# Another order for the head, the first tile's groups and the float32 pairs of a two-stage feed-forward kernel with chunked attention

## The chip, the cores and the metric

The kernel runs on one core of one Trainium2 chip. The metric is the device time of one execution in microseconds; lower is better. The profile names the engines PE (TensorE), PEld (its weight loads), DVE (VectorE), ACT (ScalarE), POOL (GpSimd) and SP (SyncE, which issues all the DMAs here).

## What is computed

The reference computes attention within chunks of 64 positions, then two feed-forward blocks on the 4608 rows of 512 that it gives:

```
scores = scale * q_c @ k_c^T, per chunk of 64, head of 64
attn = exp(scores - max) / (sum + 1e-9);  x = attn @ v_c
h = x @ w_in;  x2 = (h * cos(h)) @ w_out            (512 -> 2048 -> 512)
out = (((x2 @ w1) * (x2 @ w2)) @ w3) @ w_out2       (512 -> 1024 -> 1024 -> 512)
```

Everything is float32. The kernel splits each float32 operand of a large matmul into a rounded high part and a low part, and forms a product by three matmuls (high by high, high by low, low by high: `mm3`, lines 102 to 104).

## The kernel before

**Tiles and groups.** The 4608 rows are nine tiles of 512 (`NTILE`), and a tile is four attention blocks of 128 rows (`j`, 36 in all). The 2048 columns of h are taken 256 at a time, eight groups (`G1`). Pass 0 does groups 0 to 4 (`GA`) of every tile in turn and pass 1 the rest. The loop runs over `groups`, with index i: i = 0 to 4 is the first tile, i = 5 to 9 the second, and so on.

**A group.** For a group the kernel computes h in two halves, d and e (`stepP` and `stepQ` for the first two tiles, a seven-product scheme `Seven` later). Each half goes through a chain: a rounded copy on ScalarE (`chain_t`, line 524), a remainder on VectorE (`chain_r`, 529), absolute value and sine on ScalarE (`chain_cos`, 534 and 535), and the product h * cos(h) on VectorE (`chain_g`, 539). The next group splits this product into high and low parts (`split_g`: ScalarE, then GpSimd, 547 and 548) and multiplies it by w_out into four accumulators (`x2_mm`, in two halves e = 0 and e = 1). So group i runs the second product of group i - 1.

**The order of a group** is written out by hand in a string. Each letter is one step and every engine gets its instructions in that order: P, Q (or 1, 2, 5, 3) are the halves of h, a and c the copies, A and C the remainders, b and d the sines, B and D the products, s the split, x and y the halves of the second product, v one conversion slot, q one attention step, L, M, H, R the steps of a float32 pair, o the split of an attention tile into an operand. `ORDER0` holds for i = 0 to 3, `ORDER0E` for i = 4, `ORDER1P` and `ORDER1PE` for i = 5 to 9, later strings after that. `START` orders the head the same way: A, B, E, C, D with a block's number are its attention steps, x is a conversion slot, o an operand's split.

**Attention.** A block has five steps: A, scores on TensorE and maximum and subtraction on VectorE (`att_scores`, 343 to 347); B, the exponential on ScalarE (353); E, sums and scaling (358 to 362; the scaling is on VectorE in the head, on GpSimd later); C, four transposes and their copy `pt` (369, 371); D, the values and their copy into `xf` (383, 387). The tile `qk` has two buffers and so has the tag `ex`, which the exponentials `ex` and the copies `pt` share; `vt` has one. Step A of block j first issues the loads of q and k of block j + 1, step D those of v. The head runs blocks 0 to 3, and groups 0 to 3 of a tile run one block each of the next tile.

**Weights.** The twenty weight blocks of groups 0 to 4 come as 64-bit numbers, 512 KB each. `conv_tick` moves a pipeline by one slot: it loads a raw block two slots ahead, prepares one (`conv_a`, 120 to 122), adds the parts of another (`conv_b`, 128) and rounds and splits a third (`conv_c`, 173, and the low part at 195). Three raw buffers are in turn. One slot is about four VectorE instructions. A block is usable three slots after its preparation began, and `need` in the loop before each group makes sure that the slots so far cover what the group reads: slot t gives block t - 4, and group i needs the blocks 4i and 4i + 1 of w_in, and 2 and 3 behind them one group later.

**Float32 pairs.** From the third tile on, h uses sums and differences of weight blocks. `conv_b` stores the float32 form of w_in to the array `wr`; `sum_load` reads a pair of blocks back (207), `sum_make` forms four sums on VectorE (216 to 219), `sum_hi` and `sum_lo` split them (224, 228). There are five pairs. Before, L issues a load only when no pair is under way, and the next group's M makes it, so that a load stands one group's end ahead of its use.

Of the kernel before, what the change touches and what calls it, by code (L numbers as in the profile page):

```python
# [21 lines left out]
NJ = NT // P  # L22
# [3 lines left out]
GA = 5  # L26
# [5 lines left out]
SCALE = 0.125  # L32


START = "A0 x x A1 B0 E0 x B1 C0 E1 D0 C1 A2 x D1 A3 B2 E2 o o C2 B3 E3 D2 C3 x D3 o o"

ORDER0 = "PsvqQqacvAqCxvqbBdyvDq"
ORDER0E = "PsvQacvACxobBodyDoo"
ORDER1P = "PsqMhQqqHaclAxqbCrRmBdyqDL"
ORDER1PE = "SPsQacATCoobBoxodoDyoo"  # L40
ORDER1 = "1s2qMh5qqHa3clAxqbCrRmBdyqDL"
# [11 lines left out]
def chunk_attention_two_ffn(  # L53
# [96 lines left out]
    def new_w(key):  # L150
        W[key] = t = wpool.tile([P, 2, TT], F32R, tag=f"w{take(slots, key)}", name="w")
        return t
# [46 lines left out]
        return True  # L199


    sp = {}

    def sum_load(g):
        pair = ("in", g)
        sp["at"] = pair, new_w((pair, 2))
        nc.sync.dma_start(out=f32(W[pair, 2]), in_=wr[g])

    def sum_make():
        assert not held[0] and not held[1]  # L210
        held[1] = True
        pair, w = sp["at"]
        a, m = f32(w[:, 0]), f32(w[:, 1])
        a11, a12, a21, a22 = a[:, 0:256], a[:, 256:512], m[:, 0:256], m[:, 256:512]
        s2, s3, s4, s1 = spare[:, 0, 0:256], spare[:, 0, 256:512], spare[:, 1, 0:256], spare[:, 1, 256:512]
        nc.vector.tensor_tensor(out=s3, in0=a11, in1=a21, op=ALU.subtract)
        nc.vector.tensor_tensor(out=s1, in0=a21, in1=a22, op=ALU.add)
        nc.vector.tensor_tensor(out=s2, in0=s1, in1=a11, op=ALU.subtract)
        nc.vector.tensor_tensor(out=s4, in0=a12, in1=s2, op=ALU.subtract)
        sp["parts"] = [(W[pair, 1][:, :, 0:256], s1), (w, spare[:, 0]), (new_s4((pair, 3)), s4)]  # L220
# [5 lines left out]
    def sum_lo():  # L226
        for d, x in sp.pop("parts"):
            nc.vector.tensor_tensor(out=d[:, 1], in0=x, in1=f32(d[:, 0]), op=ALU.subtract)
        sp.pop("at")
        held[1] = False  # L230

    def need(*keys):
# [88 lines left out]
    def bank(early):  # L321
        return (ps_h.tile([P, 512], F32, tag="h", name="ps_ah") if early
                else ps_at.tile([P, 512], F32, tag="at", name="ps_at"))

    def load_qk(j):
        qks[j] = t = wk.tile([P, 2, 2 * HP, 64], F32, tag="qk", name="qk")
        nc.sync.dma_start(out=t[:, 0], in_=q[j])
        nc.sync.dma_start(out=t[:, 1], in_=k[j])
# [3 lines left out]
        nc.sync.dma_start(out=vt, in_=v[j])  # L332

    def att_scores(j, early):
        if j + 1 < NJ:
            load_qk(j + 1)
        qk = qks.pop(j)
        ps = ps_at.tile([P, 512], F32, tag="at", name="ps_s")
        s3 = ps.rearrange("p (h k) -> p h k", k=64)
        for h in range(2 * HP):  # L340
            for c in range(2):
                r = slice(64 * c, 64 * c + 64)
                nc.tensor.matmul(s3[r, h], qk[r, 0, h], qk[r, 1, h], start=True, stop=True)  # L343
        mx = small.tile([P, 2 * HP], F32, tag="mx", name="mx")
        nc.vector.reduce_max(out=mx, in_=s3, axis=AX.X)
        ex = wk.tile([P, 2 * HP, 64], F32, tag="ex", name="ex")
        nc.vector.tensor_tensor(out=ex, in0=s3, in1=mx.unsqueeze(2).to_broadcast([P, 2 * HP, 64]),
                                op=ALU.subtract)
        att[j] = ex
# [324 lines left out]

    with tc.manual_schedule():
        load_qk(0)
        for g in range(GA):
            cq.extend((nm, 2 * g + e) for nm in ("in", "out") for e in range(2))
        conv_tick()
# [4 lines left out]
        plain = ["B11", "B21", "T1", "B22"]  # L684
        for tok in START.split():
            if tok == "x":
# [6 lines left out]
        def order_of(i, nth, end):  # L693
            if i < GA:
                return ORDER0E if end else ORDER0
            if i < 2 * GA:
# [10 lines left out]
        n_sums = 0  # L707
        fq = 0
        for i in range(NG):
            if i == GA:  # L710
                sq.extend(("wo2", j) for j in range(FB2))
                for g in range(GA, G1):
                    sq.extend((nm, 2 * g + e) for nm in ("in", "out") for e in range(2))
                    lq.extend((("in", g), p_) for p_ in range(4))
                    lq.extend(("out", 2 * g + e) for e in range(2))
                lq.extend(("wo2", j) for j in range(FB2))
                sq.extend(("w3", j) for j in range(N3))
                for f in range(FB2):
                    sq.extend((nm, f) for nm in ("w1", "w2"))
                    if N3 + f < 16:  # L720
                        sq.append(("w3", N3 + f))
                    lq.extend((("w12", f), p_) for p_ in range(4))
                st_load()
            if i == iB + FOLD - 1:
                load_w3()
                load_w3()
            ps, n, g = groups[i]
            k_tile = (i - iB) // (G1 - GA)
            nth = (g, g - GA)[ps]
            end = g == (GA, G1)[ps] - 1  # L730

            def load_x(op):
                nc.sync.dma_start(out=f32(X[op]), in_=xs[k_tile][op])

            need(*((("in", g), p_) for p_ in range(2 if i < 2 * GA else 4)))
            z = Plain(("in", g)) if i < 2 * GA else Seven(
                ("in", g), (bank_h,) * 4, False, load_x if ps and end and k_tile in xs else None)
            if i:
                need(*(("out", 2 * groups[i - 1][2] + e) for e in range(2)))
            n_q = n_o = n_l = 0  # L740
            for op in order_of(i, nth, end):
                if op == "s" and i:
                    split_g(i - 1)
                elif op == "x" and i:
                    x2_mm(i - 1, 0)
                elif op == "y" and i:
                    x2_mm(i - 1, 1)
                elif op == "v":
                    conv_tick()
                elif op == "L":  # L750
                    if n_sums < GA and not sp:
                        sum_load(n_sums)
                        n_sums += 1
                elif op in "MHR":
                    if sp:
                        {"M": sum_make, "H": sum_hi, "R": sum_lo}[op]()
                elif op == "l":
                    n_l += 1
                    nxt = sq[sat[1]][0] if sat[1] < len(sq) else None
                    if ps == 0 or nxt == ("w1" if nth else "w3" if n_l > 1 else "w2"):  # L760
                        st_low()
                elif op == "m":
                    st_bits()
                elif op == "h":
                    st_hi()
                elif op == "r":
                    st_lo()
                elif op in "1253PQ":
                    getattr(z, "step" + op)()
                elif op in "ac":  # L770
                    chain_t(i, z.d if op == "a" else z.e, "ac".index(op))
                elif op in "AC":
                    chain_r(i, z.d if op == "A" else z.e, "AC".index(op))
                elif op in "bd":
                    chain_cos(i, "bd".index(op))
                elif op in "BD":
                    chain_g(i, z.d if op == "B" else z.e, "BD".index(op))
                elif op == "q":
                    if i < iA and nth < 4:
                        att_tok(steps[20 * n + 5 * nth + n_q], False)  # L780
                    elif i >= iB + FOLD and fq < 4 * FB2:
                        need(("w3", fq // 2), *(("wo2", j) for j in range(FB2)))
                        fold(fq // 4, fq % 4)
                        fq += 1
                    n_q += 1
                elif op in "ST":
                    x_sums("ST".index(op))
                elif op == "o":
                    if i < GA and not n_o:
                        x_plain()  # L790
                    x_op((z.done if i < GA or i >= 2 * GA else OPS)[n_o], n + 1 if ps == 0 else None)
                    n_o += 1
            if i >= iA:
                pump()
            if n == (NTILE - 1, NTILE - 2)[ps]:
                done_with((("in", g), p_) for p_ in range(4))
            if ps == 1:
                if nth == 0 and k_tile not in xs:
                    nc.sync.dma_start(out=xf, in_=xd[k_tile] if k_tile + 1 < NTILE else x2d[order[0]])
                if nth == 1:  # L800
                    for c in range(CC):
                        load_x2a(n, c)
# [78 lines left out]
```

## Time and profile before

| | |
|---|---|
| median of 3 runs | 1572.31 us (1569.95 to 1574.7) |
| profiled execution, device time | 1572.75 us |
| its span | 1571.0 us |
| mean granted TensorE clock | 0.982 |
| busy: PE, DVE, ACT, POOL | 96%, 70%, 49%, 17% of the span |
| first P (h of group 0) starts | 37.91 us |
| P of group 4 starts | 115.50 us |

The profiled execution is one run of the program; its device time is 1.75 us more than its span, which runs from the first to the last instruction. Each engine works through its own instructions in order, and waits at an instruction until what it needs is there. The idle time in brackets at a row of a timeline is that wait, with what ended it. An engine's share of busy time is a mean over stages that have different limits; what a change of one stage is worth is read in that stage.

### The profile page before, as it was taken

What the parts mean: (1) busy time and instruction counts of PE and PEld (TensorE: products, weight loads), DVE (VectorE), ACT (ScalarE), POOL (GpSimd) and SP (SyncE); (2) the same over time, 40 slices, a digit from 0 to 9 for tenths busy, and PEclk for the clock granted to TensorE, in tenths of its full rate; (3) what the DMA queues carried; (4) which work ended last, traced back from release to release, by engine and by line L of the source; (5) the groups of instructions that cost most, each with busy time, mean ns of one, the idle gap of its engine ahead of it and who ended that gap; (6) DMA issues with size and microseconds to landing.
All of it is one profiled execution on the core that took longest, in us unless ns stands there. A gap on an engine that the chain in (4) does not pass through costs nothing.

```text
span 1571.0 us, 28515 instructions
## 1 busy us (share of the span) xinstructions
PE 1505.1 (96%) x11340; PEld 1360.7 (87%) x11340; DVE 1105.3 (70%) x1804; ACT 771.9 (49%) x1313; POOL 263.6 (17%) x206
## 2 busy tenths in 40 slices
PE   4789989999999999999999999899999999999998
PEld 4678878888888888978889888799999999999998
DVE  5875687888888877788777776556646656566464
ACT  3666777878878776555555554312212212212121
POOL 0122212222222222221222222110000000000000
PEclk8889999999999999999999999999999999999999
DMA  6644463665646544956887887931001011011000
GB/s 202 200 145 142 152 221 127 229 210 188 225 169 211 200 130 169 363 185 218 296 292 279 281 285 255 406 114 54 21 34 55 1 54 55 1 54 42 14 28 27
DMA packets 98629, 248.80 MB, mean 158 GB/s; under 512 B 10944, under 2 KB 13760, under 8 KB 96832
## 3 DMA queue, kind: packets, MB, share of 16 engines
q1 hardware_dynamic: 98496, 246.98, 44.8%
q8 instruction: 89, 1.46, 0.4%
q14 instruction: 44, 0.36, 0.1%
HBM read 151.78 MB, written 95.16 MB: 157 GB/s over the span
## 4 chain that ended last, share of the span: by engine, by line
PE 82%; DVE 7%; DMA 5%; ACT 3%; issue 1%; SPq 1%; POOL 0%; DVEq 0%; ACTq 0%; POOLq 0%
PE acc L102 11%; PE acc L103 11%; PE ps_hh L102 11%; PE acc L104 10%; PE ps_hh L104 10%; PE ps_hh L103 10%; PE ps_aa L103 5%; PE ps_aa L102 5%; PE ps_aa L104 5%; PE ps_s L343 2%; PE ps_at L383 2%; DMA w<-sd 1%; PE ps_at L369 1%; DMA xf<-xd 1%; DMA w<-wr 1%
## 5 line engine op out<-in xcount | busy, mean ns | idle before, releaser
L548 POOL TENSOR_TENSOR g<-t,g 128x512 fp32r<-128x512 f32 x144 | 198.4, 1399 | 610.8 <-ACT g L547 514.0
L102 PE MATMUL acc<-g,w 128*128 128x512 f32 x576 | 231.9, 403 | 0.0
L103 PE MATMUL acc<-g,w 128*128 128x512 f32 x576 | 229.1, 398 | 0.1
L104 PE MATMUL acc<-g,w 128*128 128x512 f32 x576 | 228.4, 396 | 0.0
L97 ACT ACTIVATE phl<-e 128x512 fp32r<-128x512 f32 x72 | 45.5, 632 | 364.8 <-DVE e L646 356.7
L466 DVE TENSOR_TENSOR d<-x,ps_hh 128x512 f32<-128x512 f32 x134 | 91.8, 685 | 159.1 <-PE ps_hh L104 107.5
L102 PE MATMUL ps_hh<-T,w 128*128 128x256 f32 x680 | 196.5, 289 | 0.3 <-ACT x L458 0.3
L103 PE MATMUL ps_hh<-T,w 128*128 128x256 f32 x680 | 193.2, 284 | 0.0
L104 PE MATMUL ps_hh<-T,w 128*128 128x256 f32 x680 | 193.1, 284 | 0.0
L102 PE MATMUL ps_hh<-B,w 128*128 128x256 f32 x656 | 189.4, 289 | 2.9 <-DVE t L539 1.8
L103 PE MATMUL ps_hh<-B,w 128*128 128x256 f32 x656 | 186.1, 284 | 0.0
L104 PE MATMUL ps_hh<-B,w 128*128 128x256 f32 x656 | 186.0, 284 | 0.0
L102 PEld LDWEIGHTS ps_hh<-B,w 128*128 128x128 f32 x656 | 125.9, 192 | 10.1 <-DVE t L539 2.5
L102 PEld LDWEIGHTS ps_hh<-T,w 128*128 128x128 f32 x680 | 131.1, 193 | 3.3 <-ACT x L458 0.6
L103 PEld LDWEIGHTS ps_hh<-T,w 128*128 128x128 f32 x680 | 131.2, 193 | 0.6
L104 PEld LDWEIGHTS acc<-g,w 128*128 128x128 f32 x576 | 110.4, 192 | 24.0
L104 PEld LDWEIGHTS ps_hh<-T,w 128*128 128x128 f32 x680 | 131.2, 193 | 0.0
L103 PEld LDWEIGHTS ps_hh<-B,w 128*128 128x128 f32 x656 | 126.0, 192 | 4.4
L102 PEld LDWEIGHTS acc<-g,w 128*128 128x128 f32 x576 | 111.1, 193 | 20.3
L103 PEld LDWEIGHTS acc<-g,w 128*128 128x128 f32 x576 | 110.8, 192 | 20.5 <-POOL g L548 0.6
L104 PEld LDWEIGHTS ps_hh<-B,w 128*128 128x128 f32 x656 | 125.9, 192 | 0.0
L103 PE MATMUL ps_aa<-T,w 128*128 128x256 f32 x432 | 122.4, 283 | 0.4 <-DVE T L98 0.4
(136 smaller groups left out, 3618.9 us busy)
## 6 DMA issues: line engine op xcount, KB each, us to landing
w<-sd SPq DMA_DIRECT2D x63, 512.0 KB, 7.7
sd<-raw SPq DMA_DIRECT2D x104, 256.0 KB, 2.4
qk<-in_q_dram SPq DMA_DIRECT2D x36, 256.0 KB, 4.8
qk<-in_k_dram SPq DMA_DIRECT2D x36, 256.0 KB, 4.7
vt<-in_v_dram SPq DMA_DIRECT2D x36, 256.0 KB, 2.9
x2a<-x2o SPq DMA_DIRECT2D x36, 256.0 KB, 2.5
x2a<-x2a SPq DMA_DIRECT2D x36, 256.0 KB, 6.3
x2d<-x2a SPq DMA_DIRECT2D x36, 256.0 KB, 4.7
```

Of the source, the lines that this page charges most:

```text
L97: nc.scalar.activation(dst[:, 0], src, AF.Copy)
L102: nc.tensor.matmul(ps, a[0], b[0], start=first, stop=False)
L103: nc.tensor.matmul(ps, a[0], b[1], start=False, stop=False)
L104: nc.tensor.matmul(ps, a[1], b[0], start=False, stop=last)
L343: nc.tensor.matmul(s3[r, h], qk[r, 0, h], qk[r, 1, h], start=True, stop=True)
L369: nc.tensor.transpose(ps[:, P * h:P * h + P], ex[:, 2 * h:2 * h + 2].rearrange("p e k -> p (e k)"), ident)
L383: nc.tensor.matmul(o[r, h, t], vt[r, c, h], pt[r, h, t], start=True, stop=True)
L466: nc.vector.tensor_tensor(out=two(self.d), in0=self.x1.unsqueeze(1).to_broadcast([P, 2, 256]), in1=two(p26), op=ALU.add)
L548: nc.gpsimd.tensor_tensor(out=lo, in0=r, in1=f32(hi), op=ALU.subtract)
```

## The change

1. **Head.** q and k of blocks 0 and 1 are both loaded before the first conversion slot. In the head, step A of block j loads up to block j + 2, and it issues that load after its matmuls. `START` puts A of block 1 right after A of block 0, and A of block j + 2 before D of block j; it has four conversion slots instead of five.
2. **First tile's groups.** In `ORDER0` the chain of d (a, A) stands before Q, the attention step A and the second conversion slot come after it, y follows x directly, one conversion slot stands between the two products and one at the group's end, and the attention steps C and D come after x and y. `ORDER0E` puts a and A before Q and y behind x likewise.
3. **Float32 pairs.** `ORDER0E` ends with L; loads no longer wait for the pair under way (`loaded` is a list), and M makes a pair when it is two groups past the one whose number it has. Every pair is made in the same group as before, and is loaded a group earlier.

```diff
-START = "A0 x x A1 B0 E0 x B1 C0 E1 D0 C1 A2 x D1 A3 B2 E2 o o C2 B3 E3 D2 C3 x D3 o o"
-ORDER0 = "PsvqQqacvAqCxvqbBdyvDq"
-ORDER0E = "PsvQacvACxobBodyDoo"
+START = "A0 A1 x B0 E0 B1 C0 x E1 A2 D0 C1 x B2 E2 A3 D1 C2 o o B3 E3 D2 C3 x D3 o o"
+ORDER0 = "PsvaAqQvqcCqxybBdvDqvq"
+ORDER0E = "PsvaAQvcCxybBodDoooL"
...
-    sp = {}
+    sp, loaded = {}, []
...
     def sum_load(g):
         pair = ("in", g)
-        sp["at"] = pair, new_w((pair, 2))
+        loaded.append((g, pair, new_w((pair, 2))))
         nc.sync.dma_start(out=f32(W[pair, 2]), in_=wr[g])
...
-        pair, w = sp["at"]
+        _, pair, w = loaded.pop(0)
...
     def att_scores(j, early):
-        if j + 1 < NJ:
-            load_qk(j + 1)
         qk = qks.pop(j)
...
                 nc.tensor.matmul(s3[r, h], qk[r, 0, h], qk[r, 1, h], start=True, stop=True)
+        while qk_at[0] < min(NJ, j + 2 + early):
+            load_qk(qk_at[0])
...
         load_qk(0)
+        load_qk(1)
...
                 elif op == "L":
-                    if n_sums < GA and not sp:
+                    if n_sums < GA:
                         sum_load(n_sums)
                         n_sums += 1
-                elif op in "MHR":
+                elif op == "M":
+                    if loaded and i > GA + loaded[0][0]:
+                        sum_make()
+                elif op in "HR":
                     if sp:
-                        {"M": sum_make, "H": sum_hi, "R": sum_lo}[op]()
+                        {"H": sum_hi, "R": sum_lo}[op]()
```

The strings move instructions in three places that matter below.

SyncE's queue at the very start, before (qk, raw and vt are the tiles of q and k, of a raw weight block and of v; the line numbers of the changed kernel are two or three higher):

```order
L327 DMA qk_175<-in_q_dram 128x512
L328 DMA qk_175<-in_k_dram 128x512
L112 DMA raw_178<-in_w_in_dram 128x1024
L112 DMA raw_180<-in_w_in_dram 128x1024
L332 DMA vt_187<-in_v_dram 128x512
L327 DMA qk_189<-in_q_dram 128x512
L328 DMA qk_189<-in_k_dram 128x512
L112 DMA raw_217<-in_w_out_dram 128x1024
L130 DMA wr0_149<-cw_213 128x512
L112 DMA raw_225<-in_w_out_dram 128x1024
```

and in the changed kernel:

```order
L329 DMA qk_175<-in_q_dram 128x512
L330 DMA qk_175<-in_k_dram 128x512
L329 DMA qk_178<-in_q_dram 128x512
L330 DMA qk_178<-in_k_dram 128x512
L112 DMA raw_181<-in_w_in_dram 128x1024
L112 DMA raw_183<-in_w_in_dram 128x1024
L334 DMA vt_190<-in_v_dram 128x512
L329 DMA qk_209<-in_q_dram 128x512
L330 DMA qk_209<-in_k_dram 128x512
L329 DMA qk_233<-in_q_dram 128x512
L330 DMA qk_233<-in_k_dram 128x512
L112 DMA raw_244<-in_w_out_dram 128x1024
```

q and k of the second block move ahead of the two raw blocks of w_in, and those of the third and fourth ahead of the first raw block of w_out.

VectorE in group 1, from the sums of its attention block on, before (t is the chain's tile, ps_hh a half of h, cw and w a weight block in conversion):

```order
L358 TENSOR_REDUCE sm_744<-ex_700 128x8
L359 TENSOR_SCALAR sm_744<-sm_744 128x8
L361 RECIPROCAL rc_747<-sm_744 128x8
L529 SCALAR_TENSOR_TENSOR t_730<-ps_hh_702,t_730 128x512
L128 ISA cw_736<-raw_614,cw_736 128x1024
L121 TENSOR_SCALAR cw_770<-raw_676 128x512
L122 SCALAR_TENSOR_TENSOR cw_770<-raw_676,cw_770 128x512
L195 TENSOR_TENSOR w_767<-cw_671,w_767 128x512
L539 TENSOR_TENSOR t_728<-t_728,ps_hh_637 128x512
L128 ISA cw_770<-raw_676,cw_770 128x1024
L121 TENSOR_SCALAR cw_804<-raw_741 128x512
L122 SCALAR_TENSOR_TENSOR cw_804<-raw_741,cw_804 128x512
```

and in the changed kernel, from the remainder of e on:

```order
L531 SCALAR_TENSOR_TENSOR t_731<-ps_hh_694,t_731 128x512
L360 TENSOR_REDUCE sm_734<-ex_692 128x8
L361 TENSOR_SCALAR sm_734<-sm_734 128x8
L363 RECIPROCAL rc_737<-sm_734 128x8
L541 TENSOR_TENSOR t_667<-t_667,ps_hh_627 128x512
L128 ISA cw_723<-raw_605,cw_723 128x1024
L121 TENSOR_SCALAR cw_777<-raw_665 128x512
L122 SCALAR_TENSOR_TENSOR cw_777<-raw_665,cw_777 128x512
L195 TENSOR_TENSOR w_773<-cw_660,w_773 128x512
L541 TENSOR_TENSOR t_731<-t_731,ps_hh_694 128x512
L128 ISA cw_777<-raw_665,cw_777 128x1024
L121 TENSOR_SCALAR cw_795<-raw_728 128x512
```

Before, a whole conversion (lines 128, 121, 122, 195) stands between the remainder of e and the product of d. Now that product follows the sums directly, one conversion stands between the two products, and another begins right behind the second.

SyncE's queue around the first float32 pair, from the end of group 4 on, before (wr_149 is the first pair's float32 form, wr_150 the second's):

```order
L332 DMA vt<-in_v_dram 128x512
L389 DMA xd_82<-xf 128x2048
L112 DMA raw<-in_wo_dram 128x1024 x2
L327 DMA qk<-in_q_dram 128x512
L328 DMA qk<-in_k_dram 128x512
L573 DMA x2a_131<-x2o 128x512 x4
L332 DMA vt<-in_v_dram 128x512
L207 DMA w<-wr_149 128x1024
L327 DMA qk<-in_q_dram 128x512
```

and in the changed kernel:

```order
L334 DMA vt<-in_v_dram 128x512
L391 DMA xd_82<-xf 128x2048
L207 DMA w<-wr_149 128x1024
L112 DMA raw<-in_wo_dram 128x1024 x2
L329 DMA qk<-in_q_dram 128x512
L330 DMA qk<-in_k_dram 128x512
L575 DMA x2a_131<-x2o 128x512 x4
L334 DMA vt<-in_v_dram 128x512
L207 DMA w<-wr_150 128x1024
```

The load of the first pair moves from behind the end of group 5 to the end of group 4.

## Rows read from the trace of the kernel before

**Rows 1.** The page, busy time of each engine with its share of the span.

```profile
PE 1505.1 (96%) x11340; PEld 1360.7 (87%) x11340; DVE 1105.3 (70%) x1804; ACT 771.9 (49%) x1313; POOL 263.6 (17%) x206
```

**Rows 2.** TensorE's timeline, head: start us, length us, engine, line, tiles, count, [idle before <-releaser].

```profile
4.19 1.97 PE L343 MATMUL ps_s<-qk 64*64 64x64 f32 x32 [4.19 <-DMA qk<-in_k_dram]
...
10.70 1.97 PE L343 MATMUL ps_s<-qk 64*64 64x64 f32 x32 [4.54 <-DMA qk<-in_k_dram]
...
16.03 1.09 PE L369 MATMUL ps_ah<-ident,ex 128*128 128x128 f32 x4 [3.36 <-DVE ex L362]
...
29.63 1.09 PE L369 MATMUL ps_ah<-ident,ex 128*128 128x128 f32 x4 [3.75 <-DVE ex L362]
...
36.00 1.97 PE L383 MATMUL ps_ah<-pt,vt 64*64 64x64 f32 x32 [1.01 <-DMA vt<-in_v_dram]
...
37.91 0.58 PE L102 MATMUL ps_hh<-B,w 128*128 128x256 f32 x1
```

**Rows 3.** The same timeline in groups 0 to 4.

```profile
50.56 1.12 PE L369 MATMUL ps_at<-ident,ex 128*128 128x128 f32 x4 [4.79 <-POOL ex L362]
...
55.63 0.58 PE L102 MATMUL ps_hh<-B,w 128*128 128x256 f32 x1 [1.30 <-DVE t L539]
...
89.44 0.66 PE L369 MATMUL ps_at<-ident,ex 128*128 128x128 f32 x4 [3.41 <-POOL ex L362]
...
115.50 0.38 PE L102 MATMUL ps_hh<-B,w 128*128 128x256 f32 x1
```

**Rows 4.** Windows, between two last products: length, then each engine's busy time, clock, DMA.

```profile
77.27:96.19 18.92, 15.51 (x138) 13.21 (x137) 16.36 (x27) 13.22 (x22) 4.30 (x3) 0.91 0.58 180
```

**Rows 5.** VectorE's timeline in group 2.

```profile
78.47 1.52 DVE L121 TENSOR_SCALAR cw<-raw 128x512 uint32<-128x512 uint32 x1
...
93.32 0.69 DVE L539 TENSOR_TENSOR t<-t,ps_hh 128x512 f32<-128x512 f32 x1 [1.72 <-ACT t L535]
...
96.19 0.68 DVE L539 TENSOR_TENSOR t<-t,ps_hh 128x512 f32<-128x512 f32 x1
```

**Rows 6.** TensorE's timeline, two later stops.

```profile
153.80 0.65 PE L369 MATMUL ps_at<-ident,ex 128*128 128x128 f32 x4 [2.61 <-POOL ex L362]
...
229.59 0.66 PE L369 MATMUL ps_at<-ident,ex 128*128 128x128 f32 x4 [4.59 <-POOL ex L362]
```

**Rows 7.** The chain that ended last, in order of time: start us, length us.

```profile
144.61 5.21 DMA w<-wr
...
219.34 5.22 DMA w<-wr
```

**Rows 8.** VectorE's timeline at the same two places.

```profile
149.84 0.43 DVE L216 TENSOR_TENSOR spare<-w 128x256 f32<-128x256 f32 x1 [2.93 <-DMA w<-wr]
...
224.58 0.42 DVE L216 TENSOR_TENSOR spare<-w 128x256 f32<-128x256 f32 x1 [3.86 <-DMA w<-wr]
```

**Rows 9.** ScalarE's timeline, head: the first two raw weights.

```profile
7.29 0.68 ACT L120 ACTIVATE raw<-raw 128x512 int32<-128x512 uint32 x1 [5.28 <-DMA raw<-in_w_in_dram]
8.60 0.67 ACT L120 ACTIVATE raw<-raw 128x512 int32<-128x512 uint32 x1 [0.63 <-DMA raw<-in_w_in_dram]
```

**Rows 10.** DMA issues in 0 to 40: engine, count, size, median us to landing.

```profile
vt<-in_v_dram SPq DMA_DIRECT2D x5, 256.0 KB, 3.3
```

**Rows 11.** ScalarE's timeline in group 2, a table switch.

```profile
90.62 0.63 ACT L534 ACTIVATE t<-t 128x512 f32<-128x512 f32 x1
91.27 1.28 ACT L535 ACT_TABLE_LOAD   x1
92.56 0.72 ACT L535 ACTIVATE t<-t,half_pi 128x512 f32<-128x512 f32 x1
```

**Rows 12.** Windows, acc's instructions alone: y without and with a stop before it.

```profile
137.20:139.90 2.70, 2.70 (x12) 1.90 (x11) 0.00 (x0) 0.00 (x0) 1.00 0.01 3
154.50:158.70 4.20, 4.20 (x12) 2.87 (x10) 0.00 (x0) 0.00 (x0) 0.59 0.60 187
```

**Rows 13.** Raw weights from 0 to 128, issue to landing.

```profile
DMA to landing us min/median/max: 3.5/4.6/9.0
```

More of the change, by code (lines that the diff above doesn't have):

```diff
@@ L228, in sum_lo @@
             nc.vector.tensor_tensor(out=d[:, 1], in0=x, in1=f32(d[:, 0]), op=ALU.subtract)
-        sp.pop("at")
         held[1] = False
@@ L323, in bank @@
                 else ps_at.tile([P, 512], F32, tag="at", name="ps_at"))
+    qk_at = [0]
     def load_qk(j):
+        qk_at[0] = j + 1
         qks[j] = t = wk.tile([P, 2, 2 * HP, 64], F32, tag="qk", name="qk")
```

## Prediction

> **What bounds the kernel now.** The page comes first: TensorE is busy 96% of the span [rows 1], so a change can only win where TensorE waits or runs at its lower clock. The timeline of TensorE shows where that is: in the first 160 us, and once near 230. I call the parts of a group P and Q (the two halves of h), A, B, E, C, D (scores, exponential, scaling, transposes and values of an attention block) and x, y (the halves of the second product, for the group before).
>
> The head ends when the first P starts, at 37.91 [rows 2]. Until then TensorE waits for k of block 1 (4.54), twice for VectorE's scaled exponentials (3.36, 3.75) and for v (1.01). In groups 0 to 3 it stops before every C (4.79 and 3.41 in the rows shown) for GpSimd's scaling [rows 3]. GpSimd is late because VectorE is: between the last products of groups 1 and 2, VectorE is busy 16.36 of 18.92 us [rows 4], and 1.72 of the rest is a wait for a sine [rows 5]. An instruction of 0.4 us shows 1.52 there beside GpSimd's work [rows 5]. So the weight conversions, four to a group, bound these groups. Two later stops, 2.61 and 4.59 before C [rows 6], come from float32 pairs that stand in the chain of work with 5.2 us each [rows 7] and keep VectorE waiting 2.93 and 3.86 [rows 8].
>
> **The change part by part.** No arithmetic is added: the same conversions, attention steps and matmuls stand in another order. One conversion slot of the head goes. 23 slots still carry all 20 weights through their four stages, so none is missing, but each is ready one slot later.
>
> *Head.* q and k of block 1 go out third and fourth in the queue, not behind two raw weights and v. The third place landed at 7.29 [rows 9], so A of block 1 starts near 7.3 and not at 10.70 [rows 2]: 3.4 earlier. What moves back are the raws, by 0.5 MB: the first lands where the second did, 8.60 [rows 9]. VectorE takes the scores (7.3 + 2.0) to 10.7, half a conversion to 11.7, and scales block 0 in 1.8: C at 13.5, not 16.03. (Maximum, subtraction and scale together took 3.3, from 12.67 to 16.03.) Then TensorE runs A of block 2 to 16.6 and D of block 0 to 18.2. Here is a new wait: block 2's subtraction needs a buffer of "ex", of which there are two, and both are held until D of block 0 has read its own. Behind it on VectorE stand a conversion and that block's scale. The order goes on: scale of block 1 done at 17.0, subtraction of block 2 18.2 to 18.9, a conversion of 2.3, scale to 23.0, C of block 2 at 23.0 instead of 29.63. v of block 1 is issued after D of block 0 and lands 3.3 later [rows 10], at 21.5, in time for its D. From there: copy of pt, two splits and exponential 3 on ScalarE to 26.4, scale to 28.3, C and D of block 3 to 32.0, P at 32.3. **Gain 5.6.** Bounds: 2.0, if of the 2.5 at C half a microsecond is lost to later raws and the rest of the chain keeps its length; 7, if TensorE runs these small matmuls at their shorter durations.
>
> *Group 0.* The rounding and r of d come right after P; x and y do not exist yet. VectorE does a conversion, r of d, scores, a conversion, r of e, sums, a product, a conversion, the other product, some 14 us from P's start, and then the fourth conversion to 16.5. P of group 1 starts when D has run, 16.2 after P of group 0 instead of 17.7 (37.91 to 55.63, [rows 2, 3]), and its second half waits 0.6 for that conversion. **Gain 1.5.** Bounds 0 to 3.
>
> *Groups 1 to 3.* A lap is VectorE's own work, if its waits go. That work is 16.36 and some 0.3 of gaps between instructions, 16.7 [rows 4]; a conversion alone is 2.27 (93.32 to 96.19 is 2.87, less a product of 0.6, [rows 5]), so four make 9.1, the rest 4.9, and GpSimd's interference 2.7. Are the waits gone? One lap, counted from the end of the fourth conversion: VectorE has a conversion to 4.4 (stretched), r of d 5.0, scores 6.4, conversion 8.7, r of e 9.3, sums 10.35, first product 10.95, conversion 13.8, product 14.4, conversion 16.7. ScalarE has the copy of d at 3.0, the conversions' steps, a table switch, the exponential at 7.05, the copy of e at 7.6, abs, a switch, the sine of d at 10.2: before 10.35. TensorE has P to 1.5, A, Q to 6.9, x and y to 12.1 without a gap, C (GpSimd done at 11.4), D to 15.0, half of the next P to 16.4, and waits 0.3 for its weights. So nothing holds VectorE: 3 x 16.7 = 50.1 instead of 59.87 (55.63 to 115.50, [rows 3]). **Gain 9.8.** Bounds: 4.4, if 1.8 of waits stay in a lap as at the sine now; 11.9, if 0.7 of the interference falls beside products, which read one operand from PSUM.
>
> The lap rests on the table switch. The load takes 1.28 us, abs ends 0.02 before it and the sine begins 0.01 after it [rows 11]; so the sum goes by 1.28. The Trainium skill, page "ScalarE: Activation LUTs", section "What ACT_TABLE_LOAD costs", speaks against this order: it adds a drain of about 1.38 us to the load, 2.66 us for a switch, and by that the sum would be 21.8 rather than 26.6. No drain shows in these rows.
>
> *The end group* has x and y adjacent now, and one conversion more that is nearly empty; TensorE fills it before and after: **0**, bounds -1 to +1.
>
> *The float32 pairs.* Each load goes a group earlier, past v, q and k of one block on SP's queue; its issue there is under 1 us and its 512 KB travel in a group whose weights have already come. At the two stops VectorE's waits of 2.93 and 3.86 go [rows 8]. At the first, GpSimd then ends 2.93 before 153.80, and x ended 2.61 before it [rows 6]: the whole 2.61 goes. At the second 3.86 of 4.59 goes. Behind the first stop y ran at a granted clock of 0.59, twelve matmuls in 4.20 us, against 2.70 at 1.00 [rows 12] (1.00 is the level of 2.4 GHz, 0.59 a mean of it and 1.2 GHz); without the stop that loss of 1.5 goes too, and I take the same at the second. **Gain** 2.61 + 1.5 + 3.86 + 1.5 = **9.5**. Bounds 6.5 (the waits alone) and 10.2. The three other pairs made no wait.
>
> **Sum.** 5.6 + 1.5 + 9.8 + 0 + 9.5 = 26.4. The profiled execution took 1572.75, so 1546.3; the median of the runs, 1572.31, lies 0.4 below it. I forecast 1546. All low bounds together give 12, all high ones 33; as they will not all fall on one side, the forecast's own range is 1540 to 1552.
>
> **The rivals.**
> - *Conversions' loads come late.* Three conversions now follow each other on VectorE. A raw is loaded when the third conversion of a group has freed a buffer and is read in the next group's first: 1.7 + 0.6 + 2.3 + 0.6 = 5.2 us. Raws landed after 4.6 at the median, 9.0 at most [rows 13]. At 9.0 each of three laps loses 3.8, and the time is 1557. For it: q, k and v go out between them. Against: the median. Chance 0.11.
> - *The head stays a chain of VectorE and buffers*, not of q and k, and shortens by 1 only: 1551. For it: the missing third buffer. Chance 0.08.
> - *The switch of tables costs more on the path than its 1.28*: a sine later by 1.4 is 1.2 after VectorE is ready, in four groups, and the time is 1551. This is what the page above would make of it. Against: [rows 11]. Chance 0.03.
> - *It does not do what it says:* the waits come back under other names (P for the last conversion, ScalarE for the pair's sums), and at most 4 us are left: 1568 to 1573. Against: at each stop named, other work is ready. Chance 0.05.
> - *Slower.* P's second half needs the conversion that ends the group before, and on ScalarE the copy of d and the exponential stand behind the step that reads the raw. So every microsecond of a late raw stretches the whole lap. It decides from a landing of 15.6 on: 3 x (15.6 - 5.2) is the 26.4 gained and 4.7 more. At 18 the time is 1585. For it: the order on ScalarE. Against: 9.0 was the longest [rows 13]. Chance 0.04.
>
> **How the numbers follow.** The forecast has 0.69. A measurement of this kernel can tell about 0.3%, 4.7 us, from no change. The forecast and the first three rivals are faster by more: 0.91; the fourth is within, 0.05; the last is slower, 0.04. The range 1540 to 1557 takes in the forecast's range, the rivals at 1551 and most of the first.
>
> **What would show it.** Right: the first P near 32, the second near 48.5, P of the end group near 98; no idle of VectorE over 0.5 us in groups 1 to 3; C right behind y; no wait of VectorE for a float32 pair. Wrong: ScalarE or VectorE waiting for raws in groups 1 to 3, a first P after 35, laps above 18, or TensorE idle before C at the two later places.

## The result, and the profile after

The changed kernel takes 1551.30 us (median of 4 runs, 1548.34 to 1551.78), the kernel before in the same rounds 1573.28 (4 runs, 1569.95 to 1574.70). The ratio is 0.9856 with an interval of 0.9837 to 0.9876: 19.5 to 25.6 us saved. The profiled execution took 1551.62 us, span 1549.8, mean granted clock 0.986.

The page of the changed kernel, busy times, to be set beside [rows 1]:

```profile
PE 1496.6 (97%) x11340; PEld 1355.9 (87%) x11340; DVE 1106.5 (71%) x1804; ACT 772.1 (50%) x1313; POOL 263.8 (17%) x206
```

The counts are the same and VectorE's busy time is 1.2 us longer: no work went. TensorE's busy time falls by 8.5 us, with the mean granted clock up from 0.982 to 0.986: fewer matmuls ran at the lower clock. The rest of the gain is idle time.

Five marks of the program show where the time went. "Lead" is how much earlier the changed kernel reaches a mark; a stage's gain is the difference of two leads. Split n is GpSimd's split of group n's product (line 548 before, 550 after), which runs at the start of group n + 1.

| mark (start, us) | before | after | lead | the stage's gain | forecast |
|---|---|---|---|---|---|
| first P | 37.91 | 33.94 | 3.97 | head 4.0 | 5.6 |
| P of group 1 | 55.63 | 51.15 | 4.48 | group 0 0.5 | 1.5 |
| P of group 4 | 115.50 | 100.29 | 15.21 | groups 1 to 3 10.7 | 9.8 |
| P of group 5 | 126.82 | 113.22 | 13.60 | end group -1.6 | 0 |
| split 12 | 251.22 | 228.47 | 22.75 | pairs 9.1 | 9.5 |

The lead stays at 22.8 up to the split at 650.16 (672.95 before), and from the split at 749.01 (770.17) on it is 21.2; the last section reads where the 1.6 between them went.

**The head.** TensorE's timeline of the changed kernel up to the first P, which answers to [rows 2]:

```profile
4.28 3.83 PE L343 MATMUL ps_s<-qk 64*64 64x64 f32 x64 [4.28 <-DMA qk<-in_k_dram]
12.53 1.09 PE L371 MATMUL ps_ah<-ident,ex 128*128 128x128 f32 x4 [4.43 <-DVE ex L364]
...
20.55 1.15 PE L385 MATMUL ps_ah<-pt,vt 64*64 64x64 f32 x32 [1.30 <-ACT ex L355]
22.43 0.63 PE L371 MATMUL ps_ah<-ident,ex 128*128 128x128 f32 x4 [0.74 <-DVE ex L364]
27.31 1.97 PE L385 MATMUL ps_ah<-pt,vt 64*64 64x64 f32 x32 [4.25 <-DMA vt<-in_v_dram]
...
32.03 1.97 PE L385 MATMUL ps_ah<-pt,vt 64*64 64x64 f32 x32 [1.71 <-DMA vt<-in_v_dram]
33.94 0.58 PE L102 MATMUL ps_hh<-B,w 128*128 128x256 f32 x1
```

A of blocks 0 and 1 run as one row of 64 matmuls: the wait of 4.54 for k of block 1 is gone. C of block 2 stands at 22.43; before it was the C at 29.63 of [rows 2]. Seven microseconds are won there, and D behind it loses 4.25 at once, D of block 3 another 1.71: both wait for v. SyncE's queue shows why for the first:

```profile
19.09 0.38 SPq L112 DMA_DIRECT2D raw<-in_w_in_dram  x1
19.56 0.40 SPq L329 DMA_DIRECT2D qk<-in_q_dram  x1
20.01 0.45 SPq L330 DMA_DIRECT2D qk<-in_k_dram  x1
21.73 7.92 SPq L334 DMA_DIRECT2D vt<-in_v_dram  x2
```

v of block 2 is issued at 21.73, when D of block 1 has read the one buffer. Ahead of it stand 512 KB of a raw weight and 512 KB of q and k. It lands 5.5 us after its issue, at 27.2, not after the 3.3 of [rows 10]; k ahead of it lands at 26.5. v of block 3, issued at 29.3 when D of block 2 has run, lands after 2.6: D of block 3 waits for the one buffer and not for the queue. The wait of 1.30 before D of block 1 is for v too, which lands at 20.4; the exponential that the profile names is not read by that D, and in e5 below the same D starts at 18.60, ahead of it (19.30).

**The first tile's groups.** TensorE's timeline, each C and the P behind it, which answers to [rows 3]:

```profile
46.88 1.11 PE L371 MATMUL ps_at<-ident,ex 128*128 128x128 f32 x4 [3.71 <-POOL ex L364]
...
51.15 0.58 PE L102 MATMUL ps_hh<-B,w 128*128 128x256 f32 x1
...
65.64 0.60 PE L371 MATMUL ps_at<-ident,ex 128*128 128x128 f32 x4
...
80.86 0.66 PE L371 MATMUL ps_at<-ident,ex 128*128 128x128 f32 x4
...
87.02 0.39 PE L104 MATMUL ps_hh<-T,w 128*128 128x256 f32 x1 [1.72 <-DVE w L195]
...
97.93 0.60 PE L371 MATMUL ps_at<-ident,ex 128*128 128x128 f32 x4
...
100.29 0.39 PE L102 MATMUL ps_hh<-B,w 128*128 128x256 f32 x1
...
103.58 0.38 PE L104 MATMUL ps_hh<-T,w 128*128 128x256 f32 x1 [1.36 <-DVE w L195]
```

In groups 1 to 3 no C waits any more. What took the place of that wait is the second half of P, which waits for the last conversion in group 3 (1.72) and in group 4 (1.36). Windows of the three laps, between two last products of VectorE (length, then busy time of PE, PEld, DVE, ACT, POOL, then clock, DMA share, GB/s), beside [rows 4]:

```profile
49.26:66.48 17.22, 16.98 (x140) 15.41 (x140) 15.82 (x26) 13.05 (x21) 3.96 (x3) 0.82 0.62 199
66.48:82.94 16.46, 15.14 (x162) 13.33 (x164) 16.22 (x27) 14.34 (x24) 4.28 (x3) 1.00 0.64 208
82.94:99.50 16.56, 14.16 (x135) 12.43 (x133) 16.32 (x27) 13.00 (x21) 4.42 (x3) 1.00 0.67 207
```

In the last two laps VectorE is busy 16.2 to 16.3 us of 16.5: the lap is its own work now, as the 16.36 of [rows 4] had it, and only its 2.56 of idle time went. The first lap is longer, 17.22 with VectorE busy 15.82, at a granted clock of 0.82. Three of VectorE's rows, the wait that stayed and what the split does to a conversion:

```profile
63.61 0.69 DVE L541 TENSOR_TENSOR t<-t,ps_hh 128x512 f32<-128x512 f32 x1 [0.79 <-ACT t L537]
...
85.20 1.77 DVE L195 TENSOR_TENSOR w<-cw,w 128x512 fp32r<-128x512 f32 x1
86.89 1.77 DVE L128 CUSTOM_DVE_ANT_0 cw<-raw,cw 128x1024 uint16<-128x1024 uint16 x1
```

The last conversion of a group now falls beside GpSimd's split at the start of the next (84.74 to 88.1). Its line 195 takes 1.77 instead of 0.68, and P at 87.02 waits for it.

**The float32 pairs.** VectorE at the first pair of the changed kernel, beside the first of [rows 8]:

```profile
133.21 0.42 DVE L216 TENSOR_TENSOR spare<-w 128x256 f32<-128x256 f32 x1
```

and TensorE's C at the two places of [rows 6]:

```profile
137.41 0.60 PE L371 MATMUL ps_at<-ident,ex 128*128 128x128 f32 x4
...
208.44 0.66 PE L371 MATMUL ps_at<-ident,ex 128*128 128x128 f32 x4 [1.19 <-POOL ex L364]
```

No instruction waits for a pair: none of the five rows of line 216 shows idle time before it. The stops fall from 2.61 to 0 and from 4.59 to 1.19.

### The profile page after: what moved, and what is told of

The parts are those of the page before. It is cut to its first block, busy times and chain, and to the rows that moved or that the text cites. A ratio compares the mean times of both kernels' runs of the same rounds, so it can differ in the third digit from the quotient of the medians.

```text
span 1549.8 us, 28517 instructions
## 1 busy us (share of the span) xinstructions
PE 1496.6 (97%) x11340; PEld 1355.9 (87%) x11340; DVE 1106.5 (71%) x1804; ACT 772.1 (50%) x1313; POOL 263.8 (17%) x206
## 4 chain that ended last, share of the span: by engine, by line
PE 81%; DVE 8%; DMA 5%; ACT 4%; issue 1%; SPq 1%; POOL 0%; DVEq 0%; ACTq 0%; POOLq 0%
PE acc L102 10%; PE ps_hh L102 10%; PE acc L103 10%; PE acc L104 10%; PE ps_hh L104 10%; PE ps_hh L103 10%; PE ps_aa L102 5%; PE ps_aa L103 5%; PE ps_aa L104 5%; PE ps_s L343 2%; PE ps_at L385 2%; DMA w<-sd 1%; DMA xf<-xd 1%; PE ps_at L371 1%; ACT t L536 1%
## 5 line engine op out<-in xcount | busy, mean ns | idle before, releaser
L102 PE MATMUL acc<-g,w 128*128 128x512 f32 x576 | 228.7, 397 | 0.0
L103 PE MATMUL acc<-g,w 128*128 128x512 f32 x576 | 225.8, 392 | 0.1
L104 PE MATMUL acc<-g,w 128*128 128x512 f32 x576 | 225.0, 391 | 0.0
L104 PEld LDWEIGHTS acc<-g,w 128*128 128x128 f32 x576 | 108.5, 188 | 23.4
L103 PEld LDWEIGHTS acc<-g,w 128*128 128x128 f32 x576 | 109.1, 189 | 19.9 <-POOL g L550 0.6
L102 PEld LDWEIGHTS acc<-g,w 128*128 128x128 f32 x576 | 109.0, 189 | 19.8
```

Of the source, the lines that this page charges most:

```text
L102: nc.tensor.matmul(ps, a[0], b[0], start=first, stop=False)
L103: nc.tensor.matmul(ps, a[0], b[1], start=False, stop=False)
L104: nc.tensor.matmul(ps, a[1], b[0], start=False, stop=last)
```

## The experiments

Each ratio is to the kernel before, timed in the same rounds (median 1573.60 of 11 runs for the first three and e5, 1574.59 of 9 for e4, e6 and e7). "Split 12" is its start, which marks the end of what the change touches: 251.22 before, 228.47 in the changed kernel. The first three experiments put one part of the change each into the kernel before.

### e1_head: the head alone

```diff
-START = "A0 x x A1 B0 E0 x B1 C0 E1 D0 C1 A2 x D1 A3 B2 E2 o o C2 B3 E3 D2 C3 x D3 o o"
+START = "A0 A1 x B0 E0 B1 C0 x E1 A2 D0 C1 x B2 E2 A3 D1 C2 o o B3 E3 D2 C3 x D3 o o"
...
+        while qk_at[0] < min(NJ, j + 2 + early):
+            load_qk(qk_at[0])
```

with the rest of the new loading as in the change: none ahead of the scores' matmuls, and q and k of block 1 loaded at the start.

> The kernel before with the changed head alone (START, q and k two blocks ahead, loads after the scores' matmuls); group orders and float32 pairs as before. Theory: the head is worth the 4.0 us that the changed kernel's first P shows (33.94 instead of 37.91), and group 0 gives 1.4 of it back, because its first P runs at the lower clock (5.0 instead of 3.6 us): lead of the first P 4.0, lead at P of group 1 about 2.6, time 1568 to 1570. Rival (the prediction's term): the head is worth 5.6 by itself and something in the new group order takes it away: first P at 32.3, time 1567. Second rival: with four slots and the old order the conversions come late, P of groups 1 to 4 waits for weights: no faster than before.

### e2_groups: the groups' strings alone

```diff
-ORDER0 = "PsvqQqacvAqCxvqbBdyvDq"
-ORDER0E = "PsvQacvACxobBodyDoo"
+ORDER0 = "PsvaAqQvqcCqxybBdvDqvq"
+ORDER0E = "PsvaAQvcCxybBodDooo"
```

> The kernel before with the new orders of groups 0 to 4 alone; the head keeps its five conversion slots, the pairs their loads. Theory: the laps of groups 1 to 3 shrink from 59.9 to about 49 us whatever the head does, and as every weight is a slot earlier than in the changed kernel, P of group 4 waits for none and the end group takes 11.3 as before, not 12.9: 1560 to 1561. Rival: the end group's loss comes from x and y standing together there, not from the late weights; then it is lost here too: 1562 to 1563, with P of group 4 to P of group 5 at 12.9.

### e3_pairs: the pairs' loads alone

```diff
-ORDER0E = "PsvQacvACxobBodyDoo"
+ORDER0E = "PsvQacvACxobBodyDooL"
...
-                    if n_sums < GA and not sp:
+                    if n_sums < GA:
```

with the list `loaded` and the test at M as in the change.

> The kernel before with the float32 pairs' loads one group earlier, and nothing else. Theory: both stops before C go with the lower clock behind them, as in the changed kernel (4.1 and 5.0 us by its A to A distances): 1563, and VectorE waits for no pair. Rival: only the waits of 2.6 and 3.9 themselves are won and the clock stays low for another reason: 1566. Third: the earlier load at the end of group 4 delays the first raw of the next stage, whose reader then waits: less than 6 won.

| | median, us | range, runs | ratio, interval | us saved | first P | split 12 |
|---|---|---|---|---|---|---|
| head | 1568.97 | 1567.82 to 1571.38, 7 | 0.9975, 0.9964 to 0.9987 | 3.9 | 33.13 | 246.26 |
| groups | 1563.58 | 1561.23 to 1565.34, 5 | 0.9938, 0.9923 to 0.9952 | 9.8 | 37.04 | 236.56 |
| pairs | 1564.64 | 1561.64 to 1565.46, 5 | 0.9942, 0.9927 to 0.9957 | 9.1 | 37.36 | 239.04 |

The savings (one less the ratio, by 1573.6) add up to 22.8; the whole change by its ratio gives 22.7. Each of them is uncertain by 1.8 to 3.1, so an overlap of a few us would not show in the times. At split 12 it does: the leads there, 4.96, 14.66 and 12.18, add up to 31.8, and the whole change has 22.75. Part of the difference is chance. The heads of e2 and e3 are those of before, and still win 0.9 and 0.6 with the landing of k of block 1 (9.74 and 10.16, against 10.70); e3 leads by 2.25 at split 3, before anything of its change has run; and the profiled executions of e2 and e3 are the fastest of their five. Part is not: the parts meet in group 0 and in the end group, which are longer behind the new head than in e2 (17.21 from P to P for 15.84, and 12.54 for 10.92, below).

Two things more come out of them. With e2, which keeps the five conversion slots of the old head, the second half of P waits for no weight, and from split 3 to split 4, over the end group, it takes 10.92 us, as before (10.94); the changed kernel takes 12.54. So it is not the end group's new order that costs 1.6. The lost slot stands for 1.36 of it in the changed kernel's trace, as P's wait for the last conversion; e6 tests what the slot gives back. And with e1 alone the head has the same two waits for v (3.63 and 1.62): they belong to the head. What e1 was expected to show besides, that group 0 gives 1.4 us of the head back by the lower clock, did not come: its lead is 4.78 at the first P (33.13) and 4.62 at P of group 1 (51.01).

### e5_v2buf: v with a second buffer in the head

```diff
-        vs[j] = vt = one.tile([P, 2, HP, 64], F32, tag="v", name="vt")
+        vs[j] = vt = one.tile([P, 2, HP, 64], F32, tag="d" if j in (1, 3) else "v", name="vt")
...
-        if j + 1 < NJ:
-            load_v(j + 1)
+        if j + 1 < NJ and j != 2:
+            load_v(j + 1 + (j < 2))
...
         load_v(0)
+        load_v(1)
```

> The changed kernel, in the head alone v has a second buffer (blocks 1 and 3 use the space of d, idle until the third tile), v of blocks 0 and 1 is loaded at the start and v of blocks 2 and 3 one block earlier. Theory: what cut the head's gain from 5.6 to 4.0 is v's single buffer: D of block 2 waits 4.25 and D of block 3 1.71 us for a v that can only be asked for when the D before has run. With the buffer those waits go, first P near 31, lead over the changed kernel about 2.5 to 3: 1548 to 1549. Rival: the head is VectorE's chain (maximum, subtraction, scale, conversion), and D only moves its wait to the scaled exponential: first P at 33 or later, less than 1 us won. Second rival: the earlier bytes of v delay raws and k, and the head grows.

It took 1546.59 us (1546.02 to 1549.68, 5 runs), ratio 0.9834 (0.9818 to 0.9851). TensorE's timeline from D of block 1 on:

```profile
18.60 1.10 PE L385 MATMUL ps_ah<-pt,vt 64*64 64x64 f32 x32
22.08 0.63 PE L371 MATMUL ps_ah<-ident,ex 128*128 128x128 f32 x4 [2.38 <-DVE ex L364]
23.40 1.98 PE L385 MATMUL ps_ah<-pt,vt 64*64 64x64 f32 x32 [0.69 <-ACT pt L373]
27.09 1.09 PE L371 MATMUL ps_ah<-ident,ex 128*128 128x128 f32 x4 [1.72 <-DVE ex L364]
28.93 1.97 PE L385 MATMUL ps_ah<-pt,vt 64*64 64x64 f32 x32 [0.75 <-ACT pt L373]
30.83 0.58 PE L102 MATMUL ps_hh<-B,w 128*128 128x256 f32 x1
```

The waits for v are gone, that of D of block 1 too, and those for VectorE's scaled exponentials (2.38 and 1.72) are what is left: 7.26 of waits (1.30, 4.25 and 1.71) became 3.1 of gain at the first P. At split 12 the gain over the changed kernel is 4.3 (224.19).

### e4_qk5late: nothing loaded ahead of v that is not needed

```diff
-        while qk_at[0] < min(NJ, j + 2 + early):
+        while qk_at[0] < min(NJ, j + 2 + (early and j < 3)):
```

q and k of block 5 (in step A of the head's last block) are loaded a block later; v keeps its one buffer.

> The changed kernel, but q and k of block 5 are loaded at step A of block 4 as before, not at A of block 3, so that their 0.5 MB are not ahead of v of block 2 in the queue. v keeps its single buffer. It tells apart why v of block 2 landed 5.6 us after its issue and D of block 2 waited 4.25. Theory: half of that wait is bytes ahead of it: v lands in about 3.5, the wait before D of block 2 falls to about 2, first P 1.5 to 2 us earlier (near 32), time 1549 to 1550. Rival: only the single buffer matters (v cannot be asked for before D of block 1 has run): the landing stays over 5 and the first P near 34. Second rival: A of block 5 then waits for its q and k in group 1 and the gain is lost there.

It took 1546.97 us (1546.68 to 1548.20, 4 runs), ratio 0.9829 (0.9816 to 0.9843). SyncE's queue and TensorE's timeline:

```profile
19.16 0.38 SPq L112 DMA_DIRECT2D raw<-in_w_in_dram  x1
22.33 4.38 SPq L334 DMA_DIRECT2D vt<-in_v_dram  x2
```

```profile
21.15 1.15 PE L385 MATMUL ps_ah<-pt,vt 64*64 64x64 f32 x32 [2.18 <-DMA vt<-in_v_dram]
...
25.20 1.15 PE L385 MATMUL ps_ah<-pt,vt 64*64 64x64 f32 x32 [2.29 <-ACT ex L355]
27.30 1.08 PE L371 MATMUL ps_ah<-ident,ex 128*128 128x128 f32 x4 [0.95 <-DVE ex L364]
29.13 1.97 PE L385 MATMUL ps_ah<-pt,vt 64*64 64x64 f32 x32 [0.75 <-ACT pt L373]
31.03 0.58 PE L102 MATMUL ps_hh<-B,w 128*128 128x256 f32 x1
```

v of block 2 is issued 0.6 later than in the changed kernel, from the same single buffer, and lands 2.7 us after, at 25.0. TensorE still waits for v, 2.18 before D of block 1 and 2.29 before D of block 2, where the profile names an exponential that this D does not read. That costs almost nothing against e5: the next C waits for VectorE until 27.30, and in e5 until 27.09. In the changed kernel VectorE is done at 27.30 as well, and the C starts at 29.22, behind the late D. Removing 512 KB from the queue is worth as much as a buffer: split 12 starts at 224.32, in e5 at 224.19. The buffer alone was therefore not the cause; it was the buffer together with what had been queued ahead of the load. Where q and k of block 5 are ahead, the v behind them landed 0.5 to 0.7 us after that k each time: 27.2 after 26.5 in the changed kernel, 26.4 after 25.9 in e1, 26.0 after 25.4 in e6.

### e6_slot: the fifth conversion slot back

```diff
-START = "A0 A1 x B0 E0 B1 C0 x E1 A2 D0 C1 x B2 E2 A3 D1 C2 o o B3 E3 D2 C3 x D3 o o"
+START = "A0 A1 x B0 E0 B1 C0 x E1 A2 D0 C1 x B2 E2 A3 D1 C2 o o B3 E3 x D2 C3 x D3 o o"
```

> The changed kernel with a fifth conversion slot in the head, behind E of block 3, so that every weight is ready one slot earlier again; nothing else. Theory: TensorE's waits of 1.72 and 1.36 us in the second half of P of groups 3 and 4 go, because they are for the last conversion of the group before, which GpSimd's split stretches from 2.3 to 3.3; the end group takes 11.3 us instead of 12.9, and VectorE has one conversion less to do in group 3, and the head has idle time on VectorE and ScalarE for it: 2 to 3 us won, 1548 to 1549. Rival: the slot costs its 2.3 us of VectorE in the head and the first P comes later by as much: 1551 or more. Second rival: the waits for weights only hid waits for VectorE behind them (remainder of d): the waits go and the laps stay, under 1 us won.

It took 1550.19 us (1547.15 to 1551.61, 5 runs), ratio 0.9846 (0.9830 to 0.9862): no difference from the changed kernel (0.9837 to 0.9876) that can be told. P's waits of 1.72 and 1.36 are gone, and groups 1 to 3 are no shorter: from split 1 to split 3 it is 32.33 us, and 32.29 in the changed kernel. There P's wait only took up time in which VectorE was the one to be waited for. The end group gets 0.5 back (12.03 from split 3 to split 4, for 12.54) and not the 1.6 that e2 has. In the head the slot brings a raw weight's load (27.70) ahead of v of block 3 (28.13): D waits 3.20 for that v, and the first P is at 33.90 although v of block 2 lands after 3.8. TensorE before the last C, in e6 and in e2:

```profile
96.47 0.66 PE L371 MATMUL ps_at<-ident,ex 128*128 128x128 f32 x4 [1.31 <-POOL ex L364]
```

```profile
98.72 0.66 PE L369 MATMUL ps_at<-ident,ex 128*128 128x128 f32 x4 [1.31 <-POOL ex L362]
```

Both stop 1.31. Windows from the D behind it on, e6 and then e2:

```profile
97.90:112.70 14.80, 14.80 (x112) 13.73 (x113) 8.52 (x14) 9.11 (x17) 2.98 (x2) 0.88 0.63 231
```

```profile
100.20:113.50 13.30, 13.30 (x113) 12.27 (x113) 8.51 (x14) 9.11 (x17) 3.00 (x2) 1.00 0.62 218
```

The same matmuls took 14.8 us at a mean granted clock of 0.88 in the one and 13.3 at 1.00 in the other. In e7 a stop of 1.32 at the same place is followed by the slow D again (1.71; e6 1.55, e2 1.15). Why the clock fell behind two of three equal stops these runs don't say.

### e7_both: e5 and e6 together

The edits of both.

> The changed kernel with both: v's second buffer in the head and the fifth conversion slot behind E of block 3. Theory: the two gains are at different places and add: 3 to 3.5 from v and 2 to 3 from the slot, 1544 to 1546, faster than every kernel so far. Rival: with v's wait gone VectorE is the head's chain, and the slot's 2.3 us lie on it: no better than with v's buffer alone, 1547 or more.

It took 1546.01 us (1543.56 to 1547.26, 4 runs), ratio 0.9820 (0.9804 to 0.9836): the lowest median of all, and faster than both kernels, but at split 12 it stands where e5 does (224.34 and 224.19). The slot adds nothing in time here that these runs can tell. By the marks it gives 0.66 in the end group again (11.88 from split 3 to split 4, 12.54 in e5), which the head took beforehand: k of block 1 came 0.84 later than in e5 (7.25 for 6.41), and the first P 0.71 (31.54).

## Why the prediction was right, and where its steps were not

The prediction said 1546 (1540 to 1557) and faster; 1551.3 lies in the range, 5.3 above the forecast and just inside the forecast's own 1540 to 1552. The mechanism of each part was right in the main. The time came out high by a wait that was left out in two terms, a lower clock in one, and what went missing behind the change. By terms: the head lost 1.6 of its forecast, group 0 1.0, the end group 1.6, the pairs 0.4, and groups 1 to 3 gave 0.9 more. That makes 22.7 instead of 26.4, and 1.6 of it is not there at the end of the profiled execution.

- **Head: the step that failed is the landing of v.** "Lands 3.3 later" is worked out for block 1 alone, where v took 3.1, and from "copy of pt, two splits and exponential 3" on the path has nothing for v of blocks 2 and 3. v of block 2 took 5.5. The forecast does not name q and k of block 5, which stand ahead of it, and did not ask what the early loads stand ahead of. At 3.3 it would have been there at 25.0, as it is in e4, where the first P came at 31.03. The steps before it held: C of block 2 was forecast at 23.0 and came at 22.43, and the feared wait for the buffer of "ex" was 0.92 on VectorE. In e5 and e4 the first P, at 30.83 and 31.03, is 7.1 and 6.9 earlier than before: the forecast of 32.3 was then even cautious, its path too long elsewhere, so that the head missed by no more than 1.6 is in part luck.
- **Group 0: the order was right, the clock was not.** The forecast had 16.2 us from P to P. The lap took 17.21. Windows over the first 5 us from the first P on, changed kernel, then e5, before, e1 and e6:

```profile
33.90:38.90 5.00, 5.00 (x26) 4.88 (x24) 3.53 (x6) 2.86 (x5) 0.00 (x0) 0.55 0.79 270
```

```profile
30.80:35.80 5.00, 5.00 (x50) 4.84 (x50) 3.53 (x6) 3.46 (x7) 0.00 (x0) 0.72 0.65 253
```

```profile
37.90:42.90 5.00, 5.00 (x60) 4.79 (x59) 3.56 (x7) 2.85 (x5) 0.00 (x0) 0.87 0.78 291
```

```profile
33.10:38.10 5.00, 5.00 (x59) 4.77 (x57) 3.53 (x6) 2.84 (x5) 0.00 (x0) 0.83 0.79 284
```

```profile
33.90:38.90 5.00, 5.00 (x45) 4.87 (x44) 3.53 (x6) 3.32 (x6) 0.00 (x0) 0.69 0.72 292
```

  The counts take in small matmuls of the next A; P's own first 24 take 5.01, 4.25, 3.64, 3.80 and 4.42 us. Less these the lap of the new order is 12.2 in every run that has it: 17.21 here, 16.44 in e5, 16.42 in e4, 16.62 in e6, and 15.84 in e2, where the 24 take 3.65. So the whole difference is how long the first matmuls of P stay at the lower clock. That the late v lowers that clock is not shown, and e1 speaks against it: with nearly the same waits for v (3.63 and 1.62 for 4.25 and 1.71) P runs there at 0.83, in e6 with longer ones (2.34, 3.42 and 3.20) at 0.69, and in e5 with none at 0.72. What decides it these runs leave open.
- **Groups 1 to 3: right.** Forecast 50.1 for three laps, measured 49.1 from P to P. The bound was VectorE's work; it had no wait beyond 0.79, for a sine in group 1.
- **The end group: the step that failed is "0".** The working of the change had the lost slot ("each is ready one slot later") and the lap had a wait of P for it, 0.3; neither was carried into the end group. e2 shows the new order at 0, the changed kernel's trace a wait of P of 1.36 in its place, and e6 that the slot is worth 0.5 at least there. The 1.1 between e6 and e2 is the lower clock shown above.
- **Pairs: right.** The first of the two groups, from split 5 to split 6, went from 17.40 to 13.45, 3.95 against 4.1 forecast, and the second, from split 10 to split 11, from 18.87 to 13.95, 4.9 against 5.4. e3 alone gives 9.1 from split 4 to split 12.

**The rivals.** *Late raws* (1557, and the slower case) fell. Issue to landing of the raw weights in the stretch of [rows 13], changed kernel:

```profile
DMA to landing us min/median/max: 3.4/3.8/8.5
```

The only wait for one up to 128 is the head's first, 5.5. *A head of VectorE and buffers* is half true, with another buffer than the one named: v's, not that of "ex". *The switch of tables* fell too. ScalarE's timeline in group 1, which answers to [rows 11]:

```profile
60.92 0.62 ACT L536 ACTIVATE t<-t 128x512 f32<-128x512 f32 x1
61.56 1.28 ACT L537 ACT_TABLE_LOAD   x1
62.85 0.72 ACT L537 ACTIVATE t<-t,half_pi 128x512 f32<-128x512 f32 x1
```

1.28 and no gap, where it is nearest to the path (the product at 63.61 waits 0.79 for that sine). The drain that the Trainium skill, page "ScalarE: Activation LUTs", section "What ACT_TABLE_LOAD costs", adds to the load does not show here either; the measurement decides. *It does not do what it says* came true in name alone: P does wait for the last conversion, but that hid behind VectorE except in the end group.

**The signs.** Of those for "right", the marks came late (33.94, 51.15 and 100.29 for 32, 48.5 and 98), VectorE's wait of 0.79 in group 1 is over the 0.5 allowed, and C right behind y and no wait for a pair held. Of those for "wrong" one showed, TensorE idle before C at the second later place: 1.19, where the prediction's own sum leaves 0.73 (4.59 less 3.86). The sentence on the page's rule starts from a sum of 26.6; the sum was 26.4.

## What to carry to other kernels

A load that is moved ahead in a queue has to be priced by what is issued behind it soon after, not only by what it stands behind: with 512 KB of early q and k ahead of it the next v, which had one buffer and could not be issued early, took 3.8 to 5.5 us to land instead of 2.7. Where a stage is bound by one engine, waits elsewhere in it are not terms of the sum; the lap of that engine, its work without idle time, is the forecast, and it held within 1 us of 50. The clock behind a stop of TensorE belongs in the range and not in the sum: the same first 24 matmuls took 3.6 to 5.0 us here, and not by the length of the waits ahead of them.

## What was not expected of the hardware

**The clock behind a stop is not the same each time.** Far behind the change TensorE has a like stop in both executions, first the changed kernel's row and then that of before:

```profile
728.12 0.58 PE L102 MATMUL ps_hh<-B,s 128*128 128x256 f32 x1 [2.91 <-DVE d L468]
```

```profile
750.72 0.39 PE L102 MATMUL ps_hh<-B,s 128*128 128x256 f32 x1 [2.93 <-DVE d L466]
```

and the windows behind them, in the same order:

```profile
728.10:734.40 6.30, 6.28 (x27) 5.63 (x28) 5.20 (x9) 3.13 (x6) 0.00 (x0) 0.75 1.01 286
```

```profile
750.70:757.00 6.30, 6.28 (x33) 5.48 (x34) 5.89 (x11) 3.77 (x7) 0.00 (x0) 1.00 0.94 286
```

The stop is the same, the first matmul takes 0.58 in the one and 0.39 in the other, and the clock behind it is 0.75 and 1.00. The lead falls by 1.44 there (splits at 725.27 and 738.51, before at 747.87 and 759.67). Two changes ahead of it nearly cancel: 1.55 won behind a stop of 1.52 that was 2.35 before, with no lower clock behind it, and 1.95 lost at the next one, 2.96 instead of 1.02, in a stretch in which the DMA engines are fully busy in both. Together they are the 1.6 that went missing on the way to the end. A term of 1 to 2 us can therefore not be read from one profile's end; the leads at the marks are better, and carry chance too (e3 is 1.7 us further ahead at split 3 than at its first P, with nothing changed between them: behind a stop of 2.88 in both, the clock from split 2 to split 3 is 1.00 there and 0.83 before).

**GpSimd's split stretches whatever conversion is beside it, and the total stays.** Line 195 went from 0.68 to 1.77 where the new order put it beside the split, yet VectorE's work in a lap stayed at 15.8 to 16.3 us (16.36 before, [rows 4]): the interference moved to other instructions and did not shrink. The gain of 0.7 a lap that the upper bound allowed for it did not come.
